# A second load of the weights moved to ScalarE's queue, and 13 more products on zeros near the start

## The chip, the core and the metric

The kernel runs on one core of a Trainium2 chip. The time is that of the device for one execution, in microseconds. The core has five engines that run side by side and wait for one another through semaphores: TensorE (PE; its weight loads are listed apart as PEld), VectorE (DVE), ScalarE (ACT), GpSimd (POOL) and SyncE (SP). SyncE here only issues transfers. A transfer that an engine issues goes to that engine's own queue, and 16 DMA engines work on all queues.

## The reference

Two parts follow each other. First a linear attention with a decaying state, for 4 batches, 8 heads, 768 steps and a head size of 48:

```
for t in range(S):
    y[:, :, t] = einsum(r_t, state + u * k_t v_t)
    state = w_t[:, :, :, None] * state + k_t v_t
```

Then, with x the attention's output as 3072 rows of 384:

```
h = max(max(x @ w1, x @ w2), x @ w3)      # 384 -> 768, three times
out = h @ w_out                           # 768 -> 384
```

The weights arrive as 64-bit floats, the other inputs as 32-bit floats. The result is in 32-bit floats.

## The kernel before

The attention is cut into 24 units `k`: a unit is 128 steps of one batch for all heads. Each unit goes through steps that the code names with letters. On TensorE: X (`scores`, L477), T (`transposes`, L497), R (`from_state`, L508), U (`to_state`, L518), V (`values`, L547) and Y (the second half of V). On VectorE: b and f (scans, L399 and L414), r (L423), d (L434) and M (`take`, L483). On ScalarE: the copy `a` behind M (L486), copies out of PSUM (`kn` L499, `scur` L527, `sums` L451), c (a square, L428), E (the copy into x, L565), and `touch` (L553). `touch` is a copy of four columns behind V; Y waits for it, so that Y adds to sums that V has finished. On GpSimd: the two selects of e (L457).

The second part works on halves of 512 rows of x. `up` makes nine products of 128x128 by 512 columns for each of 18 tiles (L167), `down` the products with `w_out` (L201). ScalarE and VectorE take the maximum and split its result (L150, L152, L132, L133).

The order in which all this is issued is written out by hand as far as the ninth unit and beyond it: `PARTS` is a string of steps that one loop walks through, and `ORD` with the loop behind it does the rest. Each engine executes its own instructions in that order. In `PARTS`, `W4` stands for `warmer(4)`: four products of a tile of zeros, 128x128 by 512 columns in bf16 (L588), into a PSUM tile of the pool `psm` that nobody reads. The pool has four buffers that all products share, so each `W` takes a buffer as well.

The weights are loaded twice. The first load (L302) is converted to pairs of fp32 numbers: `low` (L317, L318 on ScalarE) and `weights` (L331, L342 on VectorE). It relies on the exponents of the weights lying in a certain range. The second load is for the check of that: `check_w` (L348 to L368) brings the 24 blocks of 384 KB one after the other into a single tile, `again[0]`. A call reads the block that is there on VectorE (L363), squares and sums it on ScalarE (L365), and issues the load of the next block into the same tile (L368). In the kernel before, SyncE issues that load. It has to wait until VectorE has read the tile, and what is issued behind it on SyncE waits with it: inputs of later units (`tin` L260, `kr` L246, `v` L249), rows of the output (L681), and copies within x (L573). A call comes after every third group of the second part; the calls begin near 178 us of the span.

Of the kernel before, what the change touches and what calls it, by code (L numbers as in the profile page):

```python
# [72 lines left out]

PARTS = """b0 w p0 W2 q0 d0 b1 w f0 p1 r0 e0 W11 q1 R0 d1 c0 T0 f1 X0 w e1 M0 V0 n3 r1 Y0 d2 X1 b2 U0 p2 q2 l E0 f2 c l
           M1 T1 R1 c n4 r2 e2 c1 S0 b3 W4 V1 Y1 E1 d3 p3 w X2 M2 q3 T2 f3 w U1 S1 w r3 W6 R2 c2 w W5 w V2 e3 l Y2 c3 b4
           c X3 E2 d4 M3 W3 l l R3 T3 U2 S2 n5 c gd1 V3 p4 w c l gd0 q4 f4 t r4 gd3 l Y3 w E3 c t w t l c e4 b5 gd4 t p5
           d5 q5 Z4 T4 n6 c w l gd2 gd5 l c4 X4 t f5 R4 w w U4 M4 t U3 c gc0 S4 r5 t gc3 t c gc1 S3 l b6 c p6 V4 q6 t e5
           l c5 w w Z5 X5 f6 Y4 E4 l Z6 c l c M5 c d6 gc8 gc7 t l t n7 w gd8 ge10 t w gd7 c t t b7 p7 l r6 T5 s ge11 t w  # L80
           gc4 R5 l c s n8 e6 d7 l q7 t w f7 c V5 c6 X6 T6 gd6 Y5 w U5 E5 r7 S5 s t s M6 e7 c x l R6 gc6 gc2 c t V6 l c s
           X7 Y6 t w E6 ge9 l t gc5 ge13 l b8 t c T7 w ge14 c d8 p8 w l s t q8 ge15 c M7 Z7 l ge16 t ge12 c f8 c7 t t R7
           r8 c U6 s V7 X8 s n9 t S6 s t Y7 e8 ge17 D0 E7 D1 b9 D2 p9 n10 x s Z8 c8 d9 D3 M8 s s s q9 D4 D5 D6 D7 G12 b10
           s f9 s G14 r9 T8 c9 p10 G5 t R8 n11 t U7 s s q10 U8 V8 e9 t X9 f10 Y8 S7 s E8 S8 T9 G13 Z9 Z10 G16 t b11 G15
           G3 s d10 r10 c10 t G17 R9 t e10 M9 U9 p11 s V9 t X10 Y9 t E9 d11 S9 G0 t G2 q11 t f11 T10 G1 n12 G4 M10 b12
           R10 r11 t p12 X11 V10 n13 t q12 e11 t U10 d12 t f12 Z11 Y10 G6 t t s r12 s S10 G8 s t M11 t G11 c11 t e12 s G9
           T11 G10 t E10 t b13 R11 p13 G7 q13 d13 t V11 X12 s Y11 t f13 E11 U11 H0 H1 S11 M12 r13 x c13 H2 Z13 T12 H3 n14
           Z12 H4 c12 H5 H6 H7 e13"""

ORD = "R0 V0 X1 Y0 U0 E0 b2 p2 d2 q2 | f2 n3 | S0 r2 Z2 c2 | e2 M1 | T1 | |"  # L90
FR = 4
# [17 lines left out]
def kernel(ctx: ExitStack, tc, tin, nat, u_flat, u_pair, v_t, w_flat, out, ytr):  # L109
    nc = tc.nc  # L110
# [4 lines left out]
    w_all = (w_flat[0:NW * 128 * PC].rearrange("(i p n) -> i p n", p=128, n=PC) if wide else w_flat)  # L115
# [5 lines left out]
    def room(dtype=F32):  # L121

        i = free.pop(0)
        return i, w_p.tile([128, 2, PC], dtype, name=f"w{i}")
# [95 lines left out]
    with ExitStack() as fast:  # L220
# [125 lines left out]
        again = []  # L346

        def check_w():  # L348

            nonlocal spot
            if not wide or len(again) > NW:
                return
            i = len(again)
            if i == 0:
                spot, raw = room()
                again.append(raw[:, :, :].rearrange("p a b -> p (a b)").bitcast(w_all.dtype))
            else:
                again.append(None)  # L360
                hi = again[0].bitcast(U32).rearrange("p (n t) -> p n t", t=2)[:, :, 1]
                top = cv_p.tile([128, PC], U32, name="cv")
                nc.vector.tensor_scalar(out=top[:, :], in0=hi, scalar1=27, scalar2=15,  # L363
                                        op0=ALU.logical_shift_right, op1=ALU.bitwise_and)
                nc.scalar.activation(out=top[:, :].bitcast(F32), in_=top[:, :], func=AF.Square, bias=mid_top[:, :],  # L365
                                     accum_out=wacc[:, i - 1:i])
            if i < NW:
                nc.sync.dma_start(out=again[0], in_=w_all[i])  # L368

        def split_w3(i):  # L370

# [271 lines left out]
        def judge():  # L643

            while wide and len(again) <= NW:
                check_w()

            good = cst.tile([128, BIT], F32, name="good")[:, 0:2]
            ones = cst.tile([128, BIT], F32, name="ones")[:, 0:1]
            nc.vector.memset(good[:, :], 0.0)  # L650
            nc.vector.memset(ones[:, :], 1.0)
            nc.vector.tensor_scalar(out=acc[0:112, :], in0=acc[0:112, :], scalar1=LIMIT, scalar2=None, op0=ALU.is_lt)
            nc.vector.tensor_reduce(out=good[0:112, 0:1], in_=acc[0:112, :], axis=AX.X, op=ALU.add)
            want = 112 * NK
            if wide:
                nc.vector.tensor_scalar(out=wacc[:, :], in0=wacc[:, :], scalar1=PC * 0.25, scalar2=None, op0=ALU.is_equal)
                nc.vector.tensor_reduce(out=good[:, 1:2], in_=wacc[:, :], axis=AX.X, op=ALU.add)
                want += 128 * NW
            nc.vector.tensor_tensor(out=good[:, 0:1], in0=good[:, 0:1], in1=good[:, 1:2], op=ALU.add)
            ps = ps_m.tile([128, HT], F32, name="psm")  # L660
            nc.tensor.matmul(ps[0:1, 0:1], lhsT=good[:, 0:1], rhs=ones[:, :], start=True, stop=True)
            nc.vector.tensor_scalar(out=flag[:, :], in0=ps[0:1, 0:1], scalar1=float(want), scalar2=None, op0=ALU.not_equal)
# [46 lines left out]
        acts = dict(w=load_w, l=low, c=weights, s=fix, x=split_x, t=lambda: now["catch_up"](1))  # L709
        for step in PARTS.split():  # L710
            if step in acts:
# [9 lines left out]
        while groups < GPH * NH:  # L721
            half, g = divmod(groups, GPH)
            if g == 0:
                while half not in xs:
                    unit()
                    take_x()
                begin(half)
            next(now["ups" if g < 3 * FT else "down"])
            groups += 1
            while units < min(UPH + groups * UPH // GPH, UNITS):  # L730
                unit()
                take_x()
            if groups % 3 == 0:
                check_w()
            take_x()

    rv = nc.values_load(flag[0:1, 0:1], min_val=0, max_val=1)
    with tc.If(rv != 0), ExitStack() as slow:
        pool = lambda name, bufs, **kw: slow.enter_context(tc.tile_pool(name=name, bufs=bufs, **kw))
        c1 = pool("c1", 1)  # L740
# [7 lines left out]
        with tc.For_i(0, B) as b:  # L748
            for pr in range(NP):
# [8 lines left out]
                for hh in range(2):  # L758
                    rows = slice(64 * hh, 64 * hh + 48)
                    for t, o in ((wt, pr * WS + 1), (rt, RK + pr * C), (kt, RK + (NP + pr) * C)):  # L760
                        for c in range(NCH):
                            nc.sync.dma_start(out=t[rows, c * C:(c + 1) * C],
                                              in_=tin[ds(b, 1), c, rows, o:o + C].rearrange("a p n -> (a p) n"))
                    nc.sync.dma_start(out=uc[rows, :], in_=u_pair[pr, hh])
                nc.vector.tensor_scalar(out=uk[0:112, :], in0=kt[0:112, :], scalar1=uc[0:112, :], scalar2=None, op0=ALU.mult)
                for j in range(KT):
                    with tc.For_i(0, 16) as i:
# [5 lines left out]
                        for hh in range(2):  # L773
                            nc.sync.dma_start(
                                out=vb[64 * hh:64 * hh + 48, :],
                                in_=v_t[ds(b, 1), 2 * pr + hh, ds(i + 16 * j, 1), :].rearrange("a e t -> (a e) t").broadcast_to([48, S]))
# [45 lines left out]
        with tc.For_i(0, NH) as half:  # L822
            x = xs_p.tile([128, KT, HT], F32, name="x")
# [83 lines left out]
```

## Time and profile before

| | us |
|---|---|
| time, median of 3 runs | 420.72 |
| lowest and highest of them | 419.97, 422.11 |
| the profiled execution | 421.41 |
| its span, first to last instruction | 419.70 |
| TensorE busy | 402.7 |
| VectorE, ScalarE, GpSimd busy | 267.5, 174.6, 81.6 |
| mean granted clock of TensorE | 0.98 |

1.71 us of the profiled execution lie outside the span. The granted clock is a share of TensorE's full speed: 1.00 is 2.4 GHz, 0.50 is 1.2 GHz. A wait in brackets behind an instruction is the time that its engine stood idle before it, and what ended it.

### The profile page before, as it was taken

The numbers are of one execution on the slowest core, as the hardware profiler recorded it, in microseconds if no ns is written. First come the engines' busy times: TensorE is split into PE (matmuls) and PEld (weight loads), VectorE is DVE, ScalarE is ACT, GpSimd is POOL, SyncE is SP. The second block draws the span as 40 slices with busy tenths as digits, with TensorE's granted clock in tenths as the row PEclk, the third lists the DMA queues.
The fourth block names the chain that finished last, engine by engine and source line by source line (L and its number), as shares of the span: only waits on it lengthen the run. The fifth ranks groups of instructions, "written<-read, shape, count | busy, mean of one in ns | idle before, by whom it ended". The sixth has DMA issues, their size and how long they took to land.

```text
span 419.7 us, 9360 instructions
## 1 busy us (share of the span) xinstructions
PE 402.7 (96%) x3839; PEld 332.2 (79%) x3839; DVE 267.5 (64%) x446; ACT 174.6 (42%) x401; POOL 81.6 (19%) x92
## 2 busy tenths in 40 slices
PE   8698999899999999999999999999979999999994
PEld 3566877687788888988889988889968888888893
DVE  6988999997858767456668475667357623233310
ACT  1547667654543252534433543433424432312210
POOL 3331222404026150123303122303113100000000
PEclk9969999999999999999999999999969999999998
DMA  8957895902452150473434673352744121200001
GB/s 209 316 167 239 268 287 161 288 8 54 152 164 79 38 170 18 141 239 112 135 105 162 205 248 114 134 153 79 234 150 141 40 77 58 76 3 0 0 32 53
DMA packets 23846, 55.70 MB, mean 133 GB/s; under 512 B 3281, under 2 KB 6673, under 8 KB 23793
## 3 DMA queue, kind: packets, MB, share of 16 engines
q1 hardware_dynamic: 23472, 54.61, 42.2%
q8 instruction: 32, 0.52, 0.5%
q10 hardware_dynamic: 320, 0.40, 0.3%
q14 instruction: 22, 0.17, 0.1%
HBM read 49.10 MB, written 4.72 MB: 128 GB/s over the span
## 4 chain that ended last, share of the span: by engine, by line
PE 84%; DVE 7%; DMA 3%; ACT 2%; issue 2%; SPq 1%; DVEq 0%; ACTq 0%
PE psm L167 53%; PE psm L201 14%; PE y L547 4%; PE grams L477 3%; PE y L508 3%; PE psm L518 2%; PE psm L497 2%; PE grams L201 1%; DMA w<-in_w_all_dram 1%; DMA tin<-in_tin_dram 1%; DVE gf L414 1%; DVE kr L434 1%; DVE tin L423 1%; DVE w L342 1%; PE psm L588 1%
## 5 line engine op out<-in xcount | busy, mean ns | idle before, releaser
L167 PE MATMUL psm<-x_hi,w 128*128 128x512 f32 x576 | 187.0, 398 | 0.0
L167 PEld LDWEIGHTS psm<-x_hi,w 128*128 128x128 f32 x576 | 109.3, 190 | 23.7 <-issue 0.2
L167 PE MATMUL psm<-x_lo,w 128*128 128x512 f32 x288 | 113.2, 393 | 0.0
L152 DVE TENSOR_TENSOR m<-psm,m 128x512 f32<-128x512 f32 x64 | 44.0, 689 | 73.2 <-PE psm L167 68.1
L457 POOL TENSOR_SCALAR_AFFINE_SELECT a<-sums 64x512 f32<-64x512 f32 x48 | 41.7, 869 | 211.9 <-DVE sums L453 118.1
L201 PE MATMUL psm<-w,h_hi 128*128 128x384 f32 x264 | 70.1, 362 | 0.0
L167 PEld LDWEIGHTS psm<-x_lo,w 128*128 128x128 f32 x288 | 54.7, 190 | 10.8
L201 PEld LDWEIGHTS psm<-w,h_hi 128*128 128x128 f32 x264 | 47.7, 188 | 4.9
L132 ACT CAST h_hi<-m 128x512 fp32r<-128x512 f32 x32 | 19.7, 620 | 54.2 <-DVE m L152 54.2
L201 PE MATMUL psm<-w,h_lo 128*128 128x384 f32 x116 | 38.9, 335 | 0.0
L399 DVE TENSOR_TENSOR_SCAN gf<-tin,d_bwd 112x517 f32<-112x517 f32 x24 | 32.0, 1334 | 6.2 <-DMA tin<-in_tin_dram 5.9
L167 PE MATMUL psm<-x,w 128*128 128x256 f32 (+1 forms) x126 | 33.8, 417 | 1.4 <-DVE w L342 1.0
L133 DVE TENSOR_TENSOR h_lo<-m,h_hi 128x512 fp32r<-128x512 f32 x32 | 23.6, 739 | 16.9 <-ACT h_hi L132 16.7
L547 PE MATMUL y<-a,v 64*64 64x128 f32 (+3 forms) x768 | 26.8, 255 | 7.6 <-ACT touch L553 4.9
L547 PEld LDWEIGHTS y<-a,v 64*64 64x64 f32 (+1 forms) x768 | 22.9, 131 | 11.6 <-ACT touch L553 5.6
L414 DVE TENSOR_TENSOR_SCAN gf<-tin,d_fwd 112x517 f32<-112x517 f32 x24 | 31.4, 1310 | 0.2
L423 DVE TENSOR_TENSOR tin<-tin,gf 112x1024 f32<-112x1024 f32 x24 | 30.3, 1261 | 0.1
L167 PEld LDWEIGHTS psm<-x,w 128*128 128x128 f32 x126 | 23.0, 190 | 9.0 <-issue 4.3
L428 ACT ACTIVATE gf<-gf 112x1034 f32<-112x1034 f32 x24 | 25.7, 1070 | 9.5 <-DVE tin L423 8.6
L150 ACT COPY m<-psm 128x512 f32<-128x512 f32 x32 | 18.6, 580 | 16.5 <-PE psm L167 16.4
L437 POOL TENSOR_TENSOR kr<-kr 128x384 f32<-128x384 f32 x16 | 17.2, 1077 | 37.6 <-DMA kr<-in_nat_dram 36.9
L133 DVE TENSOR_TENSOR x_lo<-x,x_hi 128x512 fp32r<-128x512 f32 x18 | 13.2, 780 | 15.1 <-ACT x_hi L132 15.1
(75 smaller groups left out, 448.7 us busy)
## 6 DMA issues: line engine op xcount, KB each, us to landing
w<-in_w_all_dram SPq DMA_DIRECT2D x48, 384.0 KB, 4.7
tin<-in_tin_dram SPq DMA_DIRECT2D x23, 448.0 KB, 5.4
v<-in_nat_dram SPq DMA_DIRECT2D x24, 288.0 KB, 5.5
kr<-in_nat_dram SPq DMA_DIRECT2D x16, 384.0 KB, 5.2
tin<-in_tin_dram SPq DMA_DIRECT2D x23, 229.7 KB, 4.5
out_dram<-m SPq DMA_DIRECT2D x22, 192.0 KB, 2.1
x<-x SPq DMA_DIRECT2D x30, 32.0 KB, 2.0
out_dram<-w SPq DMA_DIRECT2D x2, 192.0 KB, 3.9
```

The lines of the kernel that those rows point to most:

```text
L132: nc.scalar.copy(out=hi, in_=src)
L133: rest = lambda: nc.vector.tensor_tensor(out=lo, in0=src, in1=hi.bitcast(F32), op=ALU.subtract)
L150: nc.scalar.copy(out=m[:, cols], in_=ps[:, cols])
L152: nc.vector.tensor_tensor(out=m[:, cols], in0=ps[:, cols], in1=m[:, cols], op=ALU.max)
L167: nc.tensor.matmul(ps[:, cols], lhsT=wt[i][:, ct * 128:(ct + 1) * 128], rhs=x[part][:, ct, cols], start=(n == 0), stop=(n == KT * len(term ...
L201: nc.tensor.matmul(pss[tt][:, 0:DM], lhsT=ht[f][:, tok], rhs=wt[FT * 3 + f][:, :], start=(f == 0 and i == 0), stop=(f == FT - 1 and i == l ...
L399: nc.vector.tensor_tensor_scan(out=g[0:112, ::-1], data0=t[0:112, 0:WC][:, ::-1], data1=d_bwd[0:112, ::-1], initial=0.0, op0=ALU.mult, op1 ...
L414: nc.vector.tensor_tensor_scan(out=prep[k]["f"][0:112, :], data0=tbuf[k % NB][0:112, 0:WC], data1=d_fwd[0:112, :], initial=0.0, op0=ALU.mu ...
L423: nc.vector.tensor_tensor(out=both[0:112], in0=both[0:112], in1=by[0:112], op=ALU.mult)
L428: nc.scalar.activation(out=flat, in_=flat, func=AF.Square, accum_out=acc[0:112, k:k + 1])
L457: nc.gpsimd.affine_select(out=a[o:o + HC, 0:H, :], in_=cs[o:o + HC, :].unsqueeze(2).broadcast_to([HC, H, HC]), pattern=[[0, H], [1, HC]], ...
L547: nc.tensor.matmul(y[o:o + m, hh, s, HC:C] if part else y[o:o + m, hh, s, :], lhsT=natt[k][0][q:q + 64, at:at + m], rhs=p["a"][q:q + 64, o ...
```

## The change

The diff without the lines of `PARTS` that are only wrapped anew:

```
-... X0 w e1 M0 V0 n3 r1 Y0 d2 X1 ...
+... X0 w e1 M0 W4 V0 n3 r1 Y0 d2 X1 ...
-... c1 S0 b3 W4 V1 Y1 E1 d3 ...
+... c1 S0 b3 W10 V1 W3 Y1 E1 d3 ...

             if i < NW:
-                nc.sync.dma_start(out=again[0], in_=w_all[i])
+                (nc.scalar if i else nc.sync).dma_start(out=again[0], in_=w_all[i])
```

The first edit adds 4 products on zeros ahead of the first unit's V, 6 ahead of the second unit's V, and 3 between the second unit's V and Y, 13 in all. The second moves 23 of the 24 second loads from SyncE's queue to ScalarE's; each stands there directly behind the square (L365) of the block before it. The first load stays on SyncE.

TensorE, the second unit's V and Y, change against before (L547 are V and Y, L588 the zeros):

```order
 L547 MATMUL y<-a,v 64x64
 L547 MATMUL y<-a,v 48x64
+L588 LDWEIGHTS warm
+L588 MATMUL psm<-warm 128x512 [waits Activation_49]
...
 L547 MATMUL y<-a,v 64x128 [waits Activation_49]
 L547 MATMUL y<-a,v 48x128
```

Three pairs of a weight load and a product now stand between V and Y. The first of them waits for ScalarE: its PSUM buffer is the one that the transposes of the second unit had, so it needs the copy `kn` (L499) to be done.

ScalarE before, from the end of the split of the last half but one of x (`x_hi`) to `touch`:

```order
L132 CAST x_hi<-x 128x512 [waits DMAHW7_49,DMAHW2_49]
L365 ACTIVATE cv,sums<-cv,mid_top 128x384 [waits DVE_49]
L205 COPY m<-psm 128x384 [waits DMAHW4_49,PE_49]
L365 ACTIVATE cv,sums<-cv,mid_top 128x384 [waits DVE_49]
L150 COPY m<-psm 128x512 [waits DMAHW4_49,PE_49,Activation_49]
L553 COPY touch<-y 112x4 [waits PE_49]
```

ScalarE in the change, the same place:

```order
L132 CAST x_hi<-x 128x512 [waits DMAHW3_49,DMAHW0_49]
L365 ACTIVATE cv,sums<-cv,mid_top 128x384 [waits DVE_49]
L368 DMA w_2242<-in_w_all_dram 128x384 [waits DMAHW6_49]
L205 COPY m<-psm 128x384 [waits DMAHW4_49,PE_49]
L365 ACTIVATE cv,sums<-cv,mid_top 128x384 [waits DVE_49]
L368 DMA w_2242<-in_w_all_dram 128x384 [waits DMAHW5_49,DMAHW1_49]
L150 COPY m<-psm 128x512 [waits DMAHW4_49,PE_49,Activation_49]
L553 COPY touch<-y 112x4 [waits PE_49]
```

Each square is followed by a load now, and the second of the two loads stands ahead of `touch`. A load waits for the one before it into the same tile and, through the semaphore that it uses, for the older transfer that had this semaphore last (eight semaphores DMAHW0 to DMAHW7 serve all transfers in turn, SyncE's and ScalarE's alike).

SyncE before, the same place:

```order
L573 DMA x<-x 16x512 [waits DMAHW2_49]
L368 DMA w_2227<-in_w_all_dram 128x384 [waits DMAHW3_49,DVE_49]
L681 DMA out_dram<-m 128x384 [waits DMAHW4_49,Activation_49]
L260 DMA tin_108<-in_tin_dram 112x525 [waits DMAHW5_49]
L260 DMA tin_108<-in_tin_dram 112x1024 [waits DMAHW6_49,PE_49]
```

The load that stands here behind the copies within x (L573) is gone from SyncE in the change, and so is the one that was issued after the `kr` and `v` of this unit.

## Rows read from the trace of the kernel before

**Rows 1.** The page's first part: busy us, share of the span, instructions.

```profile
PE 402.7 (96%) x3839; PEld 332.2 (79%) x3839; DVE 267.5 (64%) x446; ACT 174.6 (42%) x401; POOL 81.6 (19%) x92
```

**Rows 2.** Whom TensorE waited for: us in total, times, longest.

```profile
PE y L547 <- ACT touch L553: 4.9, 5, 2.3
```

**Rows 3.** The chain that ended last, 300 to 341 us: start, us, what.

```profile
300.58 5.48 DMA w<-in_w_all_dram
...
308.15 0.91 PE y L547 x14
309.06 14.96 PE psm L167 x54
...
325.96 14.50 PE psm L167 x63
```

**Rows 4.** TensorE's timeline at two waits for `touch`: start, us, instruction, idle before it.

```profile
77.82 0.56 PE L547 MATMUL y<-a,v 64*64 64x128 f32 x16 [1.09 <-ACT touch L553]
...
308.15 0.91 PE L547 MATMUL y<-a,v 64*64 64x128 f32 x16 [2.26 <-ACT touch L553]
```

**Rows 5.** Stretches: length, busy PE, PEld, DVE, ACT, POOL, granted clock, DMA share, GB/s.

```profile
20.80:27.50 6.70, 5.79 (x86) 4.57 (x87) 6.63 (x9) 3.46 (x11) 3.06 (x2) 0.50 0.35 82
...
75.00:79.00 4.00, 2.91 (x69) 2.14 (x68) 4.00 (x5) 4.00 (x10) 3.77 (x4) 1.00 0.98 346
...
299.00:305.00 6.00, 6.00 (x56) 4.98 (x58) 1.56 (x4) 1.47 (x4) 0.46 (x1) 1.00 1.03 368
...
307.50:314.20 6.70, 6.05 (x28) 4.85 (x29) 3.54 (x7) 1.52 (x6) 0.00 (x0) 0.50 0.54 162
```

**Rows 6.** Issues of L368 and L573: ns; the landing of L368 in us.

```profile
L573 ACTq DMA_DIRECT2D x<-x x6: 522/602/847, 24.2 to 41.6; - x6
...
L368 SPq DMA_DIRECT2D w<-in_w_all_dram x24: 327/328/525, 178.4 to 351.1; - x24
...
DMA to landing us min/median/max: 2.8/3.3/5.5
```

**Rows 7.** TensorE's timeline, the first 33 us.

```profile
8.59 2.55 PE L588 MATMUL psm<-warm 128*128 128x512 bf16 x11
...
20.77 0.91 PE L547 MATMUL y<-a,v 64*64 64x128 f32 x16 [1.60 <-ACT a L486]
22.59 0.91 PE L547 MATMUL y<-a,v 64*64 64x128 f32 x16 [0.91 <-ACT touch L553]
23.27 1.52 PE L477 MATMUL grams<-tin 48*64 48x64 f32 x32
...
26.68 2.98 PE L588 MATMUL psm<-warm 128*128 128x512 bf16 x11
29.59 0.56 PE L547 MATMUL y<-a,v 64*64 64x128 f32 x16
...
31.01 0.85 PE L477 MATMUL grams<-tin 48*64 48x64 f32 x32
```

**Rows 8.** ScalarE's timeline, 20 to 23 us.

```profile
20.61 0.54 ACT L499 COPY kn<-psm 128x448 f32<-128x448 f32 x1
...
22.35 0.19 ACT L553 COPY touch<-y 112x4 f32<-112x4 f32 x1
```

**Rows 9.** VectorE's timeline, 28 to 32 us.

```profile
28.48 1.23 DVE L399 TENSOR_TENSOR_SCAN gf<-tin,d_bwd 112x517 f32<-112x517 f32 x1 [0.23 <-ACT gf L428]
31.56 0.56 DVE L331 SCALAR_TENSOR_TENSOR cv<-w,cv 128x384 uint32<-128x384 uint32 x1 [1.84 <-ACT cv L317]
```

**Rows 10.** ScalarE's timeline, a square and the next `touch`.

```profile
226.49 0.62 ACT L365 ACTIVATE cv<-cv,mid_top 128x384 f32<-128x384 uint32 x1 [1.55 <-DVE cv L363]
...
228.52 0.16 ACT L553 COPY touch<-y 112x4 f32<-112x4 f32 x1 [0.95 <-PE y L547]
```

**Rows 11.** VectorE's timeline at 306 us, and SyncE's waits (us in total, times, longest).

```profile
306.09 0.73 DVE L363 TENSOR_SCALAR cv<-w 128x384 uint32<-128x384 uint32 x1 [5.53 <-DMA w<-in_w_all_dram]
...
SPq L260 <- PE y L508: 37.5, 4, 10.9
```

More of the change, by code (lines that the diff above doesn't have):

```diff
@@ L68 @@
 XD = -2
[L76 to L88, printed above, removed]
@@ new lines @@
+PARTS = """b0 w p0 W2 q0 d0 b1 w f0 p1 r0 e0 W11 q1 R0 d1 c0 T0 f1 X0 w e1 M0 W4 V0 n3 r1 Y0 d2 X1 b2 U0 p2 q2 l E0 f2 c
+           l M1 T1 R1 c n4 r2 e2 c1 S0 b3 W10 V1 W3 Y1 E1 d3 p3 w X2 M2 q3 T2 f3 w U1 S1 w r3 W6 R2 c2 w W5 w V2 e3 l Y2
+           c3 b4 c X3 E2 d4 M3 W3 l l R3 T3 U2 S2 n5 c gd1 V3 p4 w c l gd0 q4 f4 t r4 gd3 l Y3 w E3 c t w t l c e4 b5 gd4
+           t p5 d5 q5 Z4 T4 n6 c w l gd2 gd5 l c4 X4 t f5 R4 w w U4 M4 t U3 c gc0 S4 r5 t gc3 t c gc1 S3 l b6 c p6 V4 q6
+           t e5 l c5 w w Z5 X5 f6 Y4 E4 l Z6 c l c M5 c d6 gc8 gc7 t l t n7 w gd8 ge10 t w gd7 c t t b7 p7 l r6 T5 s ge11
+           t w gc4 R5 l c s n8 e6 d7 l q7 t w f7 c V5 c6 X6 T6 gd6 Y5 w U5 E5 r7 S5 s t s M6 e7 c x l R6 gc6 gc2 c t V6 l
+           c s X7 Y6 t w E6 ge9 l t gc5 ge13 l b8 t c T7 w ge14 c d8 p8 w l s t q8 ge15 c M7 Z7 l ge16 t ge12 c f8 c7 t t
+           R7 r8 c U6 s V7 X8 s n9 t S6 s t Y7 e8 ge17 D0 E7 D1 b9 D2 p9 n10 x s Z8 c8 d9 D3 M8 s s s q9 D4 D5 D6 D7 G12
+           b10 s f9 s G14 r9 T8 c9 p10 G5 t R8 n11 t U7 s s q10 U8 V8 e9 t X9 f10 Y8 S7 s E8 S8 T9 G13 Z9 Z10 G16 t b11
+           G15 G3 s d10 r10 c10 t G17 R9 t e10 M9 U9 p11 s V9 t X10 Y9 t E9 d11 S9 G0 t G2 q11 t f11 T10 G1 n12 G4 M10
+           b12 R10 r11 t p12 X11 V10 n13 t q12 e11 t U10 d12 t f12 Z11 Y10 G6 t t s r12 s S10 G8 s t M11 t G11 c11 t e12
+           s G9 T11 G10 t E10 t b13 R11 p13 G7 q13 d13 t V11 X12 s Y11 t f13 E11 U11 H0 H1 S11 M12 r13 x c13 H2 Z13 T12
+           H3 n14 Z12 H4 c12 H5 H6 H7 e13"""
```

## The prediction

> **What bounds the kernel now.** I read the totals first, then whom TensorE waits for, then the chain of waits and the granted clock around each such wait. TensorE is busy for 96% of the span [rows 1], so the time is its work plus its pauses plus what it does at half clock. The one wait that comes back is that of Y for `touch`, 4.9 us in 5 waits, the longest 2.3 [rows 2]. The reader is to see two places.
>
> The late place is at 306 us. The chain runs there through the second load of a weight block: issued at 300.58, landed 5.48 us later, at 306.06; VectorE, which has stood for 5.53 us at its read of that block [rows 11], reads it; ScalarE squares it, copies, does `touch`; and TensorE goes on at 308.15 [rows 3] after 2.26 us of nothing [rows 4]. It had been ready at 305.89. Then the clock is at 0.50, 1.2 GHz, for the stretch from 307.5 to 314.2 [rows 5].
>
> The early place is the second unit. Before its V, TensorE stands 1.60 us, before its Y 0.91 us, and from 20.8 to 27.5 the clock is at 0.50 [rows 5, 7]. VectorE is busy nearly throughout [rows 5], but later stands 1.84 us, to 31.56, for a conversion on ScalarE [rows 9] that is queued behind `touch` of the third unit's V. So what delays that V, at 29.59 [rows 7], delays VectorE too. Between the two places TensorE shows only short pauses, so time gained early is kept.
>
> **Early products.** 4 cost 4 x 0.23 us (2.55 by 11 [rows 7]) ahead of the first V, 0.9 us in a wait for ScalarE; I cost them at nothing. The 6 ahead of the second V take 1.4 us of the 1.60 it waits anyway. The wait ends by ScalarE's copy behind M, whose inputs the change does not touch, so V stays at 20.77. The 3 behind it take 0.7 us; they need `kn`, done at 21.15 [rows 8], and V itself at full clock ends near 21.3. They end near 22.0, and `touch` ends at 22.54 [rows 8], so Y stays at 22.59. Without this cover, were `kn` late, they would cost 0.7 us.
>
> What they buy is the clock. If it stays at 1.00 (2.4 GHz), Y takes 0.56 instead of 0.91, saving 0.35. The three steps from 23.27 to 26.68 take 3.41 us at half clock; by their first (1.52 against 0.85 for the same product at 31.01) they take 1.90, saving 1.51. The 11 zeros take 2.55 instead of 2.98, saving 0.43 [rows 7]. The third V starts 2.3 us sooner, at 27.3. VectorE reaches its conversion step 1.97 us after that V now (31.56 less 29.59), which would be 29.3, but its own scan is busy until 29.71 [rows 9]. So the next bound is VectorE itself, and the front gains 31.56 - 29.71 = 1.85 us. Its bounds: 2.1 if the scan's own 0.23 us wait goes too, and nothing if the clock falls anyway.
>
> **The moved loads.** SyncE loses 23 issues, and no longer stands at them; `tin`, `kr`, `v`, the output's rows and the copies within x leave as much earlier. No one on TensorE's path waits for these, so that is worth nothing by itself. But it moves traffic: the block issued on SyncE behind six copies within x now leaves right after its square, before the burst that fills the DMA engines from 299 to 305 (share 1.03, 368 GB/s [rows 5]). 0.39 MB out of that burst is 1.1 us of it.
>
> The block that decides is the next. On ScalarE it leaves after its square, 0.62 us [rows 10], near 301.2 instead of 300.58. Its landing lies between 2.8 and 5.5 us after the issue, median 3.3 [rows 6]. With 1.1 us less ahead of it I take the median: landed at 304.5. From landing to TensorE it is now 308.15 - 306.06 = 2.09 us, and the next issue is queued ahead of `touch`: 0.33 on SyncE for this transfer, 0.52 to 0.85 on ScalarE for a smaller one [rows 6]; I take 0.45, nearer to the same transfer. TensorE goes on at 304.5 + 2.09 + 0.45 = 307.04, 1.15 us after it is ready instead of 2.26: 1.1 us gained. With the landing at either end the pause is 0.6 or 3.2 us.
>
> A pause of 1.09 us in just such a place, between the products of X and Y, left the clock at 1.00 [rows 4, 5]; pauses of 1.60 and 2.26 came with the fall. So at 1.15 I expect no fall, and that is the larger term: 54 products took 14.96 us from 309.06, and 63 at full clock 14.50 [rows 3], so 54 would take 12.43: 2.53 saved, and 0.35 at Y (0.91 against 0.56 [rows 4]): 2.9 us.
>
> The other 22 issues hold ScalarE for 0.33 to 0.85 us each. The tightest I find with `touch` behind has 0.95 us of idle time between [rows 10], so they stay hidden. VectorE may stand at later blocks, since each leaves 0.6 us later than it did; a stand of 5.53 us cost TensorE 2.26, so 3.3 us are covered: nothing.
>
> The sum: 421.41 - 1.85 - 1.1 - 2.9 = 415.6. The profiled execution is 0.7 us above the median of the three runs, inside their spread of 2.1, so I leave it there.
>
> The Trainium skill speaks against the late term. DMA: Bandwidth & Descriptors, section "Issuing engines are not separate DMA queues", says that transfers from several engines run and interleave on the same 16 DMA engines, and that issuing from another engine only saves time on the sequencer. The DMA share of 1.03 during the burst agrees with that. By this rule taken strictly the load takes its 5.5 us whichever engine issues it, which is the second rival.
>
> **Rivals.**
> First, the clock falls early all the same, because 0.2 us (1.60 - 1.4) stay idle ahead of V and 0.55 ahead of Y, or VectorE's gain is lost behind it. For it: the products of attention are short, and nothing in the trace shows what a pause in pieces does. Against it: 1.09 us in one piece did not do it [rows 4, 5]. Then the front gives nothing: 421.41 - 4.0 = 417.4.
>
> Second, the load comes no sooner: 5.5 us after the issue at 301.2 is 306.7, TensorE goes on at 309.25, the pause grows from 2.26 to 3.36, and the clock falls as it did. For it: the burst is at the DMA engines' limit. Against it: one block less in the burst, and a queue of its own. Front 1.85 gained, late place 1.1 lost: 420.7. Between it and my forecast lies a pause of some 1.7 us with the fall: 419.0.
>
> Third, slower: ScalarE is caught behind SyncE. Each load on ScalarE also waits for the older transfer that last used its semaphore, and SyncE issues most of these. If that one is a load of `tin` that itself stands for TensorE, up to 10.9 us [rows 11], ScalarE stands as long with `touch` behind it. Of this 3.3 us are covered; 7.6 of pause and 2.9 of clock remain. 415.6 + 10.5 = 426.1. It turns the result slower from a stand of about 6.3 us on: 3.3 covered, and 5.85 - 2.9 = 2.95 more until the gain is spent. Against it: in the program's order the partner of the load ahead of `touch` is the first of the two `tin` loads shown for SyncE, and that one waits for no engine.
>
> **Numbers.** Forecast 0.56, its own range 413.8 to 417; early nothing 0.14; late nothing 0.21; slower 0.09. A measurement of this kernel can tell 0.5%, 2.1 us, so faster is below 418.6 and slower above 422.8. The forecast, the first rival and a small part of the second are faster: 0.71; the rest of the second is the same: 0.20; the third is slower: 0.09. The range must hold the forecast, the first rival and most of the second, 413.3 to 420.6; that leaves out the third and the tails.
>
> **What would show it.** Early: clock 1.00 from 20 to 28 us, three zeros ending by 22.1, Y still at 22.6, the third V at 27.3 and no wait of VectorE for the conversion there. A Y later than 22.8 would show that the zeros themselves delay. Late: the load issued near 299.4 (all is 1.85 sooner) and landed within 3.5 us, the pause ahead of Y at most 1.3 us, clock 1.00 behind it. A landing of 5 us or more shows the second rival. On ScalarE an issue of L368 that waits more than 1 us shows the third. The forecast is wrong if either low stretch of the clock is still there.

## The result and the profile after

The changed kernel took 415.38 us (median of 4 runs, 415.26 to 415.89), the kernel before, beside it, 420.35 us (4 runs, 419.24 to 422.11). The ratio is 0.988, with a 95% interval of 0.984 to 0.992. The forecast was 415.6, with a range of 413.3 to 420.6. In a second comparison, with more runs (a0 below), the medians are 415.89 and 419.09, ratio 0.992 (0.989 to 0.995). So the gain is real, but between 3.2 and 5 us, by what the kernel before happens to do; why it varies is the last point on the prediction below. The ratios here and below leave out runs over 1.5% above the fastest of their kernel (among them one run of e1, 498.6 us at a clock of 0.753, and one of the kernel before, 1379.5 us) and are not simply quotients of the medians, which count every run.

The profiled execution has a span of 413.0 us (419.7 before) and took 415.36 us. First its totals, in the columns of [rows 1]:

```profile
PE 399.7 (97%) x3852; PEld 329.0 (80%) x3852; DVE 266.4 (65%) x446; ACT 174.9 (42%) x401; POOL 83.8 (20%) x92
```

With 13 more products TensorE is busy 3.0 us less: what it lost is time at half clock. Next, whom TensorE waited for (us in total, times, longest), beside [rows 2]:

```profile
PE y L547 <- ACT touch L553: 3.1, 5, 1.1
...
PE y L547 <- ACT a L486: 0.3, 1, 0.3
```

TensorE's timeline of the first 30 us (start, us, instruction, idle before it), beside [rows 7]:

```profile
12.94 1.04 PE L588 MATMUL psm<-warm 128*128 128x512 bf16 x4
14.11 0.56 PE L547 MATMUL y<-a,v 64*64 64x128 f32 x16
...
17.80 2.33 PE L588 MATMUL psm<-warm 128*128 128x512 bf16 x10
20.45 0.56 PE L547 MATMUL y<-a,v 64*64 64x128 f32 x16 [0.32 <-ACT a L486]
20.95 0.82 PE L588 MATMUL psm<-warm 128*128 128x512 bf16 x3
22.29 0.56 PE L547 MATMUL y<-a,v 64*64 64x128 f32 x16 [0.52 <-ACT touch L553]
...
24.58 2.55 PE L588 MATMUL psm<-warm 128*128 128x512 bf16 x11
27.05 0.56 PE L547 MATMUL y<-a,v 64*64 64x128 f32 x16
```

The second V and its Y stand where they stood (20.45 against 20.77 and 22.29 against 22.59; everything here is some 0.3 us early from the start on), the added zeros lie in what were pauses, and the third V comes at 27.05 instead of 29.59. VectorE's timeline, at the place of [rows 9] and at that of [rows 11]:

```profile
27.84 1.23 DVE L399 TENSOR_TENSOR_SCAN gf<-tin,d_bwd 112x517 f32<-112x517 f32 x1
29.03 0.90 DVE L331 SCALAR_TENSOR_TENSOR cv<-w,cv 128x384 uint32<-128x384 uint32 x1
...
302.51 0.73 DVE L363 TENSOR_SCALAR cv<-w 128x384 uint32<-128x384 uint32 x1 [4.16 <-DMA w<-in_w_all_dram]
```

The wait of 1.84 us at L331 is gone; the scan runs straight into it. At the late place VectorE still stands for the load, 4.16 us instead of 5.53. The chain that ended last, there (start, us, what), beside [rows 3]:

```profile
298.39 0.01 ACT cv L365
298.40 4.09 DMA w<-in_w_all_dram
302.49 0.02 issue
302.51 0.74 DVE cv L363
...
304.46 0.07 ACT touch L553
304.53 0.04 issue
304.57 0.56 PE y L547 x14
305.13 12.46 PE psm L167 x54
...
319.53 14.50 PE psm L167 x63
```

TensorE's timeline at that Y, beside [rows 4]:

```profile
304.57 0.56 PE L547 MATMUL y<-a,v 64*64 64x128 f32 x16 [0.88 <-ACT touch L553]
```

The load takes 4.09 us to land instead of 5.48, and the pause ahead of Y falls from 2.26 to 0.88 us; Y takes 0.56 instead of 0.91 and the 54 products 12.46 instead of 14.96. The stretches by granted clock (length, busy PE, PEld, DVE, ACT, POOL, clock, DMA share, GB/s), beside [rows 5]:

```profile
20.00:25.00 5.00, 4.16 (x90) 2.87 (x90) 5.00 (x7) 2.79 (x8) 3.06 (x2) 1.00 0.24 67
25.00:28.00 3.00, 3.00 (x42) 1.66 (x40) 2.93 (x5) 2.14 (x6) 0.00 (x0) 1.00 0.52 140
298.00:303.00 5.00, 5.00 (x60) 3.99 (x62) 0.84 (x3) 1.07 (x3) 1.98 (x2) 1.00 0.99 375
303.00:306.00 3.00, 2.12 (x53) 1.78 (x45) 2.93 (x6) 1.93 (x6) 0.03 (x1) 1.00 0.74 204
306.00:312.00 6.00, 6.00 (x29) 4.94 (x28) 5.05 (x9) 3.23 (x7) 0.92 (x2) 1.00 0.66 211
```

Both low stretches are gone. The `touch` of each unit is a good clock to read where time went, since each unit does it once. In the table it stands for the two profiled executions, by its start:

| from, to | before | after | gained |
|---|---|---|---|
| start to first `touch` | 15.06 | 14.74 | 0.32 |
| first to 20th `touch` (290.61; 288.41) | 275.55 | 273.67 | 1.88 |
| 20th to 21st (307.94; 304.36) | 17.33 | 15.95 | 1.38 |
| 21st to 22nd (325.02; 318.59) | 17.08 | 14.23 | 2.85 |
| 22nd to the end of the span | 94.7 | 94.4 | 0.3 |
| outside the span | 1.71 | 2.36 | -0.65 |

### The profile page after: what moved, and what is told of

The parts are those of the page before. It is cut to its first block, busy times and chain, and to the rows that moved or that the text cites. A ratio compares the mean times of both kernels' runs of the same rounds, so it can differ in the third digit from the quotient of the medians.

```text
span 413.0 us, 9387 instructions
## 1 busy us (share of the span) xinstructions
PE 399.7 (97%) x3852; PEld 329.0 (80%) x3852; DVE 266.4 (65%) x446; ACT 174.9 (42%) x401; POOL 83.8 (20%) x92
## 4 chain that ended last, share of the span: by engine, by line
PE 82%; DVE 9%; DMA 3%; issue 3%; ACT 2%; SPq 1%; ACTq 0%; DVEq 0%
PE psm L167 53%; PE psm L201 15%; PE y L547 3%; PE grams L477 3%; PE y L508 3%; PE psm L518 2%; PE grams L201 2%; PE psm L497 1%; DVE gf L414 1%; DVE gf L399 1%; DVE tin L423 1%; DMA tin<-in_tin_dram 1%; DMA w<-in_w_all_dram 1%; DVE w L342 1%; DVE kr L434 1%
## 5 line engine op out<-in xcount | busy, mean ns | idle before, releaser
L167 PE MATMUL psm<-x_hi,w 128*128 128x512 f32 x576 | 185.1, 395 | 0.0
L167 PEld LDWEIGHTS psm<-x_hi,w 128*128 128x128 f32 x576 | 108.1, 188 | 23.1 <-issue 0.2
L133 DVE TENSOR_TENSOR h_lo<-m,h_hi 128x512 fp32r<-128x512 f32 x32 | 22.4, 702 | 16.9 <-ACT h_hi L132 16.7
L547 PE MATMUL y<-a,v 64*64 64x128 f32 (+3 forms) x768 | 25.7, 247 | 3.6 <-ACT touch L553 3.1
L547 PEld LDWEIGHTS y<-a,v 64*64 64x64 f32 (+1 forms) x768 | 21.9, 126 | 8.4 <-ACT touch L553 4.2
L437 POOL TENSOR_TENSOR kr<-kr 128x384 f32<-128x384 f32 x16 | 18.6, 1162 | 34.0 <-DMA kr<-in_nat_dram 33.1
```

The costliest lines, as they stand in the source:

```text
L133: rest = lambda: nc.vector.tensor_tensor(out=lo, in0=src, in1=hi.bitcast(F32), op=ALU.subtract)
L167: nc.tensor.matmul(ps[:, cols], lhsT=wt[i][:, ct * 128:(ct + 1) * 128], rhs=x[part][:, ct, cols], start=(n == 0), stop=(n == KT * len(term ...
L547: nc.tensor.matmul(y[o:o + m, hh, s, HC:C] if part else y[o:o + m, hh, s, :], lhsT=natt[k][0][q:q + 64, at:at + m], rhs=p["a"][q:q + 64, o ...
```

## The experiments

All times are medians, beside runs of the kernel before on the same chip: 31 runs, median 418.49, for e1 to e4; 35 runs, 419.09, for a0, e5, e6 and e8; 17 runs, 420.14, for e9, e10, e12 and e13. "Clock" is the mean granted clock of a run's span.

**One half of the change at a time.** e1: the new order of steps, the loads back on SyncE.

```diff
-(nc.scalar if i else nc.sync).dma_start(out=again[0], in_=w_all[i])
+nc.sync.dma_start(out=again[0], in_=w_all[i])
```

> The kernel after with the second loads back on SyncE: only the 13 products on zeros are left. Theory (the front and the late place are two separate gains): clock 1.00 from 20 to 28 us, the third V near 27.1 and the conversion step of VectorE near 29.0, as in the kernel after; then the late place as in the kernel before, some 2.2 us sooner: the load that decides lands about 5.5 us after its issue, TensorE stands 2.26 us there and the clock falls to 0.50. Time: 420.35 - 2.2 = 418.1 us. Rival (the front's gain is eaten by the wait for that load, since what decides it, VectorE and the DMA queues, need not move with TensorE): the pause at the late place grows to about 4.4 us and the time is that of before, 420.3.

e2: the loads on ScalarE, the order of steps of before (the same two places of the diff, the other way round).

> The kernel before with the second loads issued by ScalarE: no added products on zeros. Theory: the early place as before (clock 0.50 from 20.8 to 27.5, third V near 29.6), the late place as in the kernel after: the load lands about 4.1 us after its issue, the pause is 0.9 us, clock 1.00 behind it, 54 products in 12.46 us. Time: 420.35 - 1.38 - 2.5 - 0.35 = 416.1 us. Rival (the late gain needs the front: at a clock that was never low the same pause does no harm): the pause is 0.9 us and the clock falls all the same, 420.35 - 1.4 = 419.0.

e1 took 418.33 us, ratio 0.996 (0.994 to 0.999); e2 417.48, ratio 0.998 (0.995 to 1.001). The chain of e1 at the late place:

```profile
299.00 5.52 DMA w<-in_w_all_dram
...
307.13 14.05 PE psm L167 x54
```

There the late place is that of before: landing after 5.52 us, a pause of 2.27, and the 54 products slow. The time came out as the theory had it (418.1), but its base did not: the kernel before took 418.5 here, not 420.35. Against it the front alone brought 0.2 us by the medians, and by the ratio 0.4% (1.5 us, with an interval of 0.3 to 2.7). TensorE's timeline of e2 shows why it can be so little:

```profile
15.26 0.91 PE L547 MATMUL y<-a,v 64*64 64x128 f32 x16 [0.29 <-ACT touch L553]
...
20.95 0.56 PE L547 MATMUL y<-a,v 64*64 64x128 f32 x16 [0.28 <-ACT a L486]
...
27.54 0.56 PE L547 MATMUL y<-a,v 64*64 64x128 f32 x16
```

With the old order of steps the clock fell here too, but at 15 us instead of 20.8 (Y 0.91 at 15.26), and was back by 20.95. What it cost lay in the wait ahead of the second V, and the third V came at 27.54, 0.5 us later than in the kernel after, of which 0.3 is from the start. So between these profiles the front's worth is 0.2 to 1.9 us, by where the clock falls without it. In other executions it is worth more: e2's profiled run, at 416.16 us, is among its fastest, its median lies 1.6 us above that of the kernel after (415.89 in a0 below), and its slowest run took 420.77 us. e2's late place is as the theory had it: landing after 4.36 us, pause 1.00, clock 1.00.

**Which part of the loads' move helps.** e3 moves load 16 alone, the one that the late place waits for; e4 load 15 alone, the one before it, which on SyncE stands behind the six copies within x.

```diff
-(nc.scalar if i else nc.sync).dma_start(...)
+(nc.scalar if i == 16 else nc.sync).dma_start(...)
```

> The kernel after with one load alone on ScalarE, number 16, the one whose landing the late place waits for; all other second loads are back on SyncE, number 15 thus behind the six copies within x and inside the burst. Theory A (relief, the prediction's step: what helped is that load 15 left the burst): number 16 lands 5.2 to 5.5 us after its issue as before, pause about 2.2 us, clock 0.50 behind it, time about 418.1. Theory B (a queue of its own: number 16 no longer stands behind SyncE's tin, kr, v and output transfers): it lands after 4.1 us or less, pause about 0.9, clock 1.00, time about 415.4.

```diff
-(nc.scalar if i else nc.sync).dma_start(...)
+(nc.scalar if i == 15 else nc.sync).dma_start(...)
```

> The kernel after with one load alone on ScalarE, number 15, the one ahead of the one whose landing the late place waits for; number 16 is issued by SyncE as in the kernel before. Theory A (relief: what helped is that number 15 leaves before the burst): number 16 lands 4.1 to 4.4 us after its issue, pause 0.9 to 1.2, clock 1.00, time about 415.4. Theory B (a queue of its own for number 16): it lands 5.2 to 5.5 us after its issue as before, pause about 2.2 us, clock 0.50, time about 418.1.

e3 took 418.15 us, ratio 0.997 (0.993 to 1.000); e4 415.24, ratio 0.991 (0.987 to 0.995). The chain of e3, and then that of e4, at the late place:

```profile
299.04 5.83 DMA w<-in_w_all_dram
...
307.14 12.47 PE psm L167 x54
```

```profile
298.60 3.85 DMA w<-in_w_all_dram
...
305.11 12.46 PE psm L167 x54
```

TensorE's timeline at the Y that waits, in e1, e3 and e4 in this order:

```profile
306.57 0.56 PE L547 MATMUL y<-a,v 64*64 64x128 f32 x16 [2.27 <-ACT touch L553]
306.58 0.56 PE L547 MATMUL y<-a,v 64*64 64x128 f32 x16 [2.25 <-ACT touch L553]
304.55 0.56 PE L547 MATMUL y<-a,v 64*64 64x128 f32 x16 [0.64 <-ACT touch L553]
```

This settles it for theory A. With a queue of its own but load 15 still in the burst, load 16 lands after 5.83 us, no sooner than on SyncE (5.52), and the pause is 2.25. With load 15 gone from the burst and load 16 on SyncE, it lands after 3.85 us and the pause is 0.64. The relief is worth 5.52 - 3.85 = 1.67 us. The other profiles agree: load 16 lands after 5.48 to 5.83 us where SyncE issues load 15 behind the copies (before, e1, e3, e5), and after 3.81 to 4.36 us where ScalarE issues it (after, a0, e2, e4, e8, e9, e12, e13), whichever queue has load 16. What no run parts is how the relief comes about: load 15's own 0.39 MB leave earlier, and SyncE, without load 15 to issue, also issues `tin`, `kr` and `v` some 0.5 us earlier ahead of load 16 (`tin` 4.01 us ahead of it in e4, 3.53 in e1). One thing missed: in e3's profile the clock stayed at 1.00 behind a pause of 2.25 us; over its ten runs the clock lies between 0.988 and 0.999.

**The kernel after once more, and load 15 alone once more.** The first is the kernel after unchanged, the second e4 again.

> The kernel after once more, beside as many runs of the kernel before as the first study had (there 31 runs gave 416.1 to 423.1 us, median 418.5, with mean granted clocks of 0.972 to 0.992, and the time rises by 2.9 us for each 0.01 of clock). Theory (the change takes away both the wait and the chance of a fall of the clock): 415.4 us, clock 0.996 or more in nearly every run, all runs within 1.5 us. Rival (the first four runs were lucky in their clock): runs at 417 to 420 with clocks below 0.99 turn up, median above 416.5.

> The kernel with the new front and load 15 alone on ScalarE, once more and beside the kernel after. In the first study its profiled span was 413.1 us, that of the kernel after 413.0, but its time lay 1.9 us above its span and that of the kernel after 2.4. Theory (the 22 other loads on ScalarE give nothing, and cost some 0.5 us outside the span): 414.9 to 415.0, some 0.4 us below the kernel after, same span. Rival (the difference of 0.5 us is one of chips or of single runs): the same time as the kernel after.

The kernel after took 415.89 us (12 runs, 415.18 to 416.98, clock 0.994 to 0.998), e8 415.48 (12 runs, 414.93 to 416.40), both with a median span of 413.5. The theory of a0 nearly held: clock and spread are a little wider than it said, but no run comes near 417.5, while before spread from 416.1 to 422.6 in the same comparison, with clocks of 0.972 to 0.996. The other 22 loads on ScalarE give the span nothing, as e8's theory said. Its 414.9 us were not reached, since the span was 0.4 us longer than assumed. The time outside the span has a median of 2.41 us in a0 and 1.83 in e8, with ranges that overlap (2.05 to 2.51 and 1.68 to 2.50); that is all of the 0.4 us between the two.

**The pause and the clock apart.** e5: the new front, all loads on SyncE, 9 products on zeros ahead of the Y that waits.

```diff
 def values_more(k):
-    values(k, 1)
+    k == 20 and warmer(9); values(k, 1)
```

> The kernel with the new front and all second loads on SyncE, and 9 products on zeros (some 2.05 us) ahead of the Y of the unit that waits at the late place: the wait for the load stays, TensorE does not stand idle in it. It parts the pause from the clock behind it. Theory (the pause is what lowers the clock): Y starts as late as without the zeros, 306.6, idle time ahead of it 0.2 to 0.3 us, clock 1.00 behind it in every run; time 416.7, which is where the runs of the front-only kernel point to for a clock of 1.00 (418.3 with a mean clock of 0.995). Rival 1 (the clock falls for another reason, such as the DMA burst): 418.3 as without. Rival 2 (the zeros themselves delay, by waiting for a free psm buffer or by holding one): Y later than 306.8, time above 418.3.

416.80 us (12 runs, 416.26 to 417.65, clock 0.993 to 0.999), ratio 0.995 (0.992 to 0.998). TensorE's timeline there:

```profile
303.98 2.12 PE L588 MATMUL psm<-warm 128*128 128x512 bf16 x9
306.51 0.56 PE L547 MATMUL y<-a,v 64*64 64x128 f32 x16 [0.41 <-ACT touch L553]
```

Y starts as late as in e1 (306.57 there), but the clock behind it stays up (1.00 from 306 to 320 us in the profiled execution), and the time is the 416.7 of the theory. Over the runs, the lowest mean clock is 0.993 instead of 0.991 in e1, and the longest time 417.65 us instead of 419.08. So it is TensorE's idleness that lowers the clock, not the burst of transfers, which is the same. Of the 2.85 us between the medians of e1 and e8, 1.5 are the clock (e1 to e5) and 1.3 the pause (e5 to e8). The first of these two spans two comparisons, whose medians of before differ by 0.6 us.

**Which gaps of the front matter.** e6 is the kernel after with only the 10 zeros ahead of the second V; e13 has load 15 alone on ScalarE and only the 4 zeros ahead of the first V.

```diff
-... e1 M0 W4 V0 n3 ... b3 W10 V1 W3 Y1 ...
+... e1 M0 V0 n3 ... b3 W10 V1 Y1 ...      (e6)
+... e1 M0 W4 V0 n3 ... b3 W4 V1 Y1 ...    (e13)
```

> The kernel after without two of the three front pieces: no products on zeros ahead of the first V and none between V and Y of the second unit; the 10 ahead of the second V stay. Theory (every front gap counts, since the loads-only kernel showed the fall already behind the first V, at 15.3 us): clock below 1.00 behind the first V or behind the second in part of the runs, mean clock about 0.992, median about 1 us above the kernel after. Rival (the pause of 1.6 us ahead of the second V was the whole cause): time and clock as the kernel after, 415.4 and 0.998.

> Load 15 alone on ScalarE, and of the 13 added products on zeros only the 4 ahead of the first V; ahead of the second V stand 4 as in the kernel before, between it and its Y none. Theory (each gap is a chance of a fall by itself): no fall at 15 us, but one behind the second V, near 21 us, in a part of the runs, where the kernel before showed it in its profile; mean clock about 0.990, median 1 us or more above the kernel with all 13 (415.5). Rival (it is the first gap that decides, and a clock that stayed up there stays up): 415.5 and 0.997 as with all 13.

e6 took 418.36 us (12 runs, 415.15 to 419.27, clock 0.984 to 0.994), e13 417.23 (12 runs, 415.70 to 418.05, clock 0.989 to 0.994). Both theories hold, and e6 is worse than its theory. Its timeline of TensorE:

```profile
15.21 0.91 PE L547 MATMUL y<-a,v 64*64 64x128 f32 x16 [0.29 <-ACT touch L553]
...
20.24 4.45 PE L588 MATMUL psm<-warm 128*128 128x512 bf16 x10
24.62 0.79 PE L547 MATMUL y<-a,v 64*64 64x128 f32 x16
```

The fall at 15 us was cheap in e2, because a wait ahead of the second V took it up. Here the 10 zeros stand in that wait and run at half clock, 4.45 us instead of 2.33; they end some 4 us after V could have started (20.45 in the kernel after). The `touch` of the second unit comes 3.25 us later than in e8 (25.54 against 22.29), and 3.15 of it are still there at the 20th (292.20 against 289.05). Zeros that do not keep the clock are a cost of their own. And e13, whose profiled run was its fastest, with a clock of 0.994 (the other eleven have 0.989 to 0.991):

```profile
20.76 0.56 PE L547 MATMUL y<-a,v 64*64 64x128 f32 x16 [1.60 <-ACT a L486]
22.58 0.56 PE L547 MATMUL y<-a,v 64*64 64x128 f32 x16 [1.27 <-ACT touch L553]
22.96 1.34 PE L477 MATMUL grams<-tin 48*64 48x64 f32 x32
```

Without a fall at 15 us the pauses of 1.60 and 1.27 us around the second V bring it on at 22.96. So each gap is a chance of a fall by itself: e6 shows that the 4 zeros ahead of the first V matter (its fall comes before the place of the 3), and e13 that the 6 and the 3 around the second V do, taken together. Whether the 6 and the 3 are each needed is not shown, since no run leaves out one of them alone.

The fall at 15 us came only behind a pause that the change does not touch. Ahead of the first unit's transposes (L497), near 11 us, TensorE stands 1.36 to 1.76 us in seven of the fourteen profiled executions (a0, e1, e2, e3, e6, e10, e12) and at most 0.72 us in the others. The clock fell between 12 and 20 us only in executions with the long pause: in both without the 4 zeros (e2, e6), and in one of the five with them (a0). Few as these are, they speak for the 4 zeros lowering the chance of that fall without taking it away. Why the pause differs from one execution to the next stays open.

**Does VectorE bound the front?** e12: load 15 alone on ScalarE, 5 of the 11 zeros ahead of the third V left out.

```diff
-... W6 R2 c2 w W5 w V2 e3 ...
+... W6 R2 c2 w w V2 e3 ...
```

> The new front with load 15 alone on ScalarE, and 5 of the 11 products on zeros ahead of the third V left out (1.16 us at full clock). Since these 11 end just at that V, at 27.3, and ScalarE's copy that it needs is done at 26.3, the V can start up to 0.95 us sooner. Theory (VectorE bounds the front, as the prediction has it: it works there without a pause from 20 to 31 us): the third V moves up by 0.9 us, the steps of VectorE and all behind them stay, time 415.5 as with them. Rival 1 (TensorE still bounds the front): 414.6. Rival 2 (the gap that opens lowers the clock): clock below 1.00 between 26 and 35 us in part of the runs, time 416 or more.

415.52 us (6 runs, 414.31 to 416.38), clock 0.997 or more. TensorE's timeline:

```profile
27.02 0.56 PE L547 MATMUL y<-a,v 64*64 64x128 f32 x16
...
28.78 0.56 PE L547 MATMUL y<-a,v 64*64 64x128 f32 x16 [0.64 <-ACT touch L553]
```

Against the start of its second V (21.35; 20.71 in e8) the third V is 0.92 us sooner (5.67 against 6.59), but its Y now waits 0.64 us, and the third `touch` stands where it stood (5.63 us behind the second; 5.64 in e8). Nothing is gained: it is not TensorE that bounds the front there. That it is VectorE, as the theory had it, is not shown: VectorE has no pause from 18 to 32 us, but the third `touch` stands behind ScalarE's own steps, which follow one another without a pause from 26.60 us, when ScalarE has issued three copies within x (2.13 us of issue, to 26.55).

**Time outside the span.** e9: the loads 1 to 11 and 15 on ScalarE.

```diff
+(nc.scalar if 0 < i < 12 or i == 15 else nc.sync).dma_start(...)
```

> The new front, and 12 of the second loads on ScalarE: numbers 1 to 11 and number 15; the rest on SyncE. It is about the time outside the span, which was 1.7 to 1.9 us for kernels with at most one of these loads on ScalarE and 2.4 us for those with 23. Theory (each load on ScalarE's queue costs its share of the 0.6 us): 2.1 us outside the span, time some 0.3 us above the kernel with load 15 alone (415.5), so 415.8. Rival 1 (only the late ones cost, near the end of the program): 1.8 us, 415.5. Rival 2 (any use beyond a few costs all): 2.4 us, 416.1.

415.21 us (4 runs, 414.79 to 415.48), 1.7 to 1.9 us of it outside the span: rival 1 is nearest. With all 23 loads on ScalarE it is 2.05 to 2.54 us in each of 40 runs (the kernel after, a0, e2, e6). But single runs of e1, e3, e8, e10 and e12, with one such load or none there, have 2.3 to 2.5 as well (2 of 11 in e1, 3 of 6 in e12), so the 1.7 to 1.9 us that the expectation starts from did not hold for every run of e1 and e3. What decides it stays open.

**A version that follows from e4: the load earlier instead of on another queue.** e10: the new front, all loads on SyncE; in the loop over the groups the check stands ahead of the units of attention.

```diff
+            if groups % 3 == 0:
+                check_w()
             while units < min(UPH + groups * UPH // GPH, UNITS):
                 unit()
                 take_x()
-            if groups % 3 == 0:
-                check_w()
             take_x()
```

> The new front, all second loads on SyncE, and each step of the check written ahead of the units of attention of its group instead of behind them. So VectorE reads block 15 ahead of the split of x, and load 16 leaves some 4 us sooner, in the middle of the burst. Theory (the late wait is a matter of when the load leaves, not of the queue): number 16 lands near 300, ahead of TensorE's need at 303; the pause ahead of the Y of that unit falls from 0.8 to 0.3 us or less, clock 1.00 behind it, time outside the span 1.8: 415.5 - 0.6 = 414.9 us. Rival (the checks now stand ahead of the unit's own steps on VectorE and ScalarE and delay these elsewhere): new waits of a Y for touch of over 0.5 us at other units, time 416 or more.

414.44 us (6 runs, 413.93 to 415.08), ratio 0.987 (0.983 to 0.991), median span 412.6: the lowest median of all the kernels here, with no load moved to ScalarE. VectorE's timeline, and then TensorE's:

```profile
300.96 0.36 DVE L363 TENSOR_SCALAR cv<-w 128x384 uint32<-128x384 uint32 x1 [2.05 <-DMA w<-in_w_all_dram]
```

```profile
303.06 0.86 PE L477 MATMUL grams<-tin 48*64 48x64 f32 x32
303.73 0.52 PE L547 MATMUL y<-a,v 64*48 64x128 f32 x16
```

The load leaves at 296.07, 2.5 us sooner than in e4 (not 4 as expected: on SyncE it stands behind the copies and `tin`), is read at 300.96, and Y follows the product of X without a pause. Load 15 leaves ahead of the copies here too (287.57; the copies start at 290.25), so this run moves both loads. The rival's new waits did not come: Y's waits for `touch` are 2.2 us in 4.

## Why the prediction was right, step by step

**Early products: right.** They cost nothing where they stand: the first V has no wait ahead of it, the 10 end before ScalarE's copy, the 3 end at 21.8 (forecast: 22.0), and Y stays. The clock is at 1.00 from 20 to 28. The next bound is VectorE: its conversion step follows its scan at once. Forecast 1.85 us, measured 1.88 from the first to the 20th `touch`. That holds against an execution with the fall at 20.8 us; against e2's, with the fall at 15 us, the same stretch gains 0.18.

**The pause at the late place: right in its mechanism, three terms mis-sized.** Forecast 1.1 us, measured 1.38. The load was to leave 0.62 us after the read, behind its square; it left 0.01 us after the square began. It was to land in the median of 3.3 us; it took 4.09, beyond the 3.5 that was to be a sign of the forecast, so the burst was relieved, not gone. Its issue was to delay `touch` by 0.45; from landing to TensorE it is 304.57 - 302.49 = 2.08 us, as before (2.09), so it cost nothing. The errors are -0.6, +0.8 and -0.45, and nearly cancel, so that 1.1 came out near 1.38 is in part luck. The upper end of the pause, 3.2, should read 3.35 by its own terms (301.2 + 5.5 + 2.54 - 305.89); the sum does not use it. That the relief comes from the block ahead, which leaves before the burst, is what e3 and e4 show; its size was 1.67 us, not 1.1. The 0.24 us between 4.09 here and 3.85 in e4 say nothing of the load's own queue: e8, the same kernel as e4, has 4.04.

**The clock at the late place: right.** Forecast 2.9, measured 2.85: 2.50 for the 54 products and 0.35 for Y. e5 shows that it is the idleness that brings the fall. The ground that the prediction gave is weaker than its result: it took the length of one pause as the sign (1.09 us without a fall, 1.60 and 2.26 with one), but e12 has no fall behind 1.76 us and e3 none behind 2.25. A short pause makes a fall rarer; that none came here is borne out by 16 runs of this kernel with clocks of 0.994 or more, and not by that rule.

**The sum.** 1.88 + 1.38 + 2.85 = 6.11 us, and 0.6 at the start and the end that belong to no step; 0.65 more outside the span took that back. So 415.36 against 415.6 is partly luck of these last two.

**The rivals.** The first, the clock falling all the same, did not come in the profiled execution: the pieces of 0.32 and 0.52 us that stay idle did no harm. In a0's a short fall is still there, between 12 and 20 us (clock 0.78 and 0.80), behind the long pause near 11 us. By the 20th `touch` 0.25 us of it is left: a0 is there 1.20 us behind the kernel after (289.61 against 288.41), and had been 0.95 behind at the first added zeros (13.89 against 12.94), ahead of the fall. The second is what e3 is: another queue and no relief, and the load lands after 5.83 us, at 418.15. There the rule from the Trainium skill (DMA: Bandwidth & Descriptors, "Issuing engines are not separate DMA queues") held as strictly as it is written: ScalarE's queue brought the load no sooner, 5.83 us against 5.52. It spoke against the term only where I let it stand for the whole move. Moving an issue to another engine also changes when the transfer leaves, since it is no longer behind what its old engine stands at, and that was the gain: load 15 left before the six copies instead of behind them. The third rival did not come either; no issue on ScalarE was held (its waits for semaphores took 0.02 us each), and VectorE's waits for the loads went from 12.5 us in 3 to 7.6 in 3.

**Where the base was weak.** The forecast was made against an execution with a fall of the clock at both places, as if these belonged to the kernel. They follow its pauses in some executions and not in others: over 82 runs of the kernel before the mean clock lies between 0.972 and 0.996, the time between 416.1 and 423.1, and the time is 2.7 to 2.9 us longer for each 0.01 that the clock is lower (correlations of -0.92 to -0.94). The profiled execution, at 0.980 and 421.41 us, is among the slower ones. The medians of before were 418.5, 419.1 and 420.1 in the three comparisons; against the first of these the gain to 415.4 is 3.1 us, not 5. So the forecast time was right, while the gain of 5.8 us that it came from was that against one of the longer executions.

## What to carry to other kernels

Ask of a late transfer first what left ahead of it: taking the one in front out of a burst, or issuing both earlier in program order, helped here, and another engine's queue by itself did not. A pause of TensorE costs its length and, in some executions, a stretch at half clock behind it; so read the spread of the runs and their mean clocks before the profile of one of them is taken as the base. Products on zeros paid here where they filled a wait but for 0.3 to 0.5 us and the clock was still up when they began; behind a gap that had lowered it they outlasted the wait (e6: 4.45 us instead of 2.33).

## What the runs showed of the hardware

ScalarE's sequencer issued a DMA while an ACTIVATE was running, and ahead of one that stands before it in the program. So the written order holds on ScalarE for the steps that compute, and an issue can run ahead of them. Its timeline in the kernel after (ACTq: its sequencer):

```profile
289.41 0.59 ACT L565 COPY x<-y 112x512 f32<-112x512 f32 x1 [0.84 <-PE y L547]
289.43 0.34 ACTq L368 DMA_DIRECT2D w<-in_w_all_dram  x1
290.00 0.62 ACT L365 ACTIVATE cv<-cv,mid_top 128x384 f32<-128x384 uint32 x1
...
298.39 0.62 ACT L365 ACTIVATE cv<-cv,mid_top 128x384 f32<-128x384 uint32 x1 [1.20 <-DVE cv L363]
298.40 0.33 ACTq L368 DMA_DIRECT2D w<-in_w_all_dram  x1
```

The square at L365 stands ahead of L368 in the program; the issue is done at 289.77, before that square begins at 290.00. What the load waits for, VectorE's read of the block, had been done by 287.32. At 298.40 the 0.33 us of issue lay wholly beside the square, which ran to 299.01.

A queue of its own gave a load no better share of a full set of DMA engines: 5.83 us on ScalarE's queue (e3) against 5.52 on SyncE's (e1) in the same burst. And the clock's falls differ between executions that pause alike at the late place: a pause of 2.25 us had none behind it in e3's profile, one of 2.27 us had one in e1's.
